# Attention stack of four layers on one core: four-head row tiles for the scores, column tiles for the sums over keys, the reciprocal of the denominators through DRAM, and the layers interleaved

## The chip, the cores and the metric

The kernel runs on one core of one Trainium2 chip. The metric is the device time in microseconds of one execution of the whole program. The engines are called PE (TensorE, matrix products), ACT (ScalarE), DVE (VectorE), POOL (GpSimd) and SP (SyncE, which here issues DMA transfers); "PEld" is PE's weight load. A matrix product has a stationary operand, the weights, and a moving one that is streamed past it.

The kernel before was run in every batch of experiments as well and gave 2697.99 to 2701.73 us in all of them, so times of different batches are compared here, but not differences of some 10 us and less.

## The reference, cut to what matters

There are 2048 tokens of width 512 and 32 heads of 16. Four layers follow each other, A, B, A, B, each on a normalised input and with a residual. A works on four segments of 512 tokens, causally, and adds a memory term; B attends to all keys.

```python
def _A_ref(x, wq, wk, wv, wo, beta):           # 4 segments s of L = 512 tokens
    phi = lambda t: jnp.where(t > 0, t + 1.0, jnp.exp(t))
    g = _sigmoid(beta).reshape(1, H, 1, 1)
    ...
    for s in range(N):
        qs, ks, vs = (q[:, :, s].copy(), k[:, :, s].copy(), v[:, :, s].copy())
        logits = jnp.einsum('bhqd,bhkd->bhqk', qs, ks) * scale + mask   # causal
        p = _softmax(logits, axis=-1)
        a_dot = jnp.einsum('bhqk,bhkd->bhqd', p, vs)
        pq = phi(qs)
        num = jnp.einsum('bhld,bhde->bhle', pq, M)
        den = jnp.einsum('bhld,bhd->bhl', pq, z)[..., None] + 1e-06
        o = g * (num / den) + (1.0 - g) * a_dot
        outs.append(o)
        pk = phi(ks)
        M = M + jnp.einsum('bhld,bhle->bhde', pk, vs)
        z = z + jnp.einsum('bhld->bhd', pk)
    ...
def _B_ref(x, wqkv, wo):
    ...
    scores = jnp.einsum('bhqd,bhkd->bhqk', q, k) * Dh ** (-0.5)
    p = _softmax(scores, axis=-1)
    o = jnp.einsum('bhqk,bhkd->bhqd', p, v)
...
x = x + _A_ref(_layernorm(x), ...); x = x + _B_ref(_layernorm(x), ...)   # twice
```

Softmax is taken without a maximum in both kernels: the exponential of all scores, the sum of exponentials times values, and a division by the sum of exponentials, which comes as a 17th column of the values, set to one.

## The kernel before: the parts that the change touches

Each layer is finished before the next begins. A head has only 16 of the 128 rows of a block of q, so the kernel masks q to one head and multiplies full 128-row blocks. The scores come out with keys on partitions and 512 queries on the free axis.

```python
    def qm_chunk(self, pair_idx, h, col0):           # q with all heads but h set to 0
        ...
        sc.add("dve", lambda e: e.tensor_scalar(dst, src, mcol, None, op0=ALU.mult), ...)

    KT_GROUPS = [[0, 1, 2], [3, 4, 5], [6, 7, 8], [9, 10, 11], [12, 13], [14, 15]]

    def b_unit(self, p, h, qc, g, slot_qm, c, uctr):
        ...
        for i, kt in enumerate(kts):                 # 3 or 2 blocks of 128 keys
            lhsT = self.kT[:, c, kt * 128:(kt + 1) * 128]
            out_ap = self.ps[:, bank.col0:bank.col0 + 512]
            sc.add("pe", ... e.matmul(out_ap, lhsT, qmap, start=True, stop=True) ...)
        ...
        sc.add("act", lambda e: e.activation(dst, src, ACT.Exp, scale=float(SCALE)), ...)
```

For the values, the exponentials are the weights: 128 keys by 128 queries are loaded, and only 17 columns are streamed. Queries then lie on partitions, so the reciprocal is of a small tile, 128x4.

```python
    def b_pv_part(self, p, h, qc, qt, state):
        ...
        for kt in range(16):
            lhsT = self.pT[:, col + qt * 128: col + (qt + 1) * 128]
            rhs = self.v_aug[:, kt, h * 17:(h + 1) * 17]
            out_ap = self.ps[:, col0 + qt * 17: col0 + (qt + 1) * 17]
            sc.add("pe", ... e.matmul(out_ap, lhsT, rhs, start=(kt == 0), stop=(kt == 15)) ...)

    def b_norm(self, p, h, qc, state):
        ...
        sc.add("dve", lambda e: e.reciprocal(sm[:, 0:4], den), ...)
        sc.add("dve", lambda e: e.tensor_tensor(dst, acc3[:, :, 0:16], rb, ALU.mult), ...)
```

The layers are built one after the other; the normalisation, the projections and, in A, the whole memory state come before the layer's first exponential.

```python
    def layer_A(self, li):
        self.ln_all(evac_eng=self.ln_evac_eng)
        for n in range(4):
            for g in self.proj_groups_A(n, nb_all):
                g()
        self.a_mem_init()
        ...                                          # a_nd_tile, a_deltaM: memory of all segments
        for s in range(NSEG):
            for h in range(H):
                info = self.a_pair(pair, s, h)       # scores, mask by a matmul, exponential
                if prev is not None:
                    self.a_pv_norm(prev)
                ...
```

## Time and profile before

| | before |
|---|---|
| time, median of 2 runs | 2701.17 us (2700.76 to 2701.58) |
| span of the profiled run | 2698.6 us |
| ACT busy | 2346.2 us (87%) |
| PE busy, instructions | 2085.3 us (77%), 26524 matmuls |
| mean granted PE clock | 0.965 |

The page gives the busy time of each engine with its share of the span and its number of instructions, then the span in 40 slices: each digit is the busy share of a slice in tenths, and for PEclk the granted clock in tenths of full speed. The page of the kernel before:

```profile
...
PE 2085.3 (77%) x26524; PEld 1242.5 (46%) x26976; DVE 777.9 (29%) x2571; ACT 2346.2 (87%) x2098; POOL 13.5 (1%) x19
...
PE   6788688777777777777786886887777777777777
...
ACT  6488658999999999999873886689999999999997
...
PEclk9799899999999999999977997999999999999998
...
```

ACT is at 9 tenths through both B layers and falls at the start of every layer. The groups by shape of the kernel before (line, engine, operation, output from input, shapes, count, then busy us, mean ns of one, and the idle time before them with what ended it):

```profile
...
L794 ACT ACTIVATE pT<-ps 128x1536 bf16<-128x1536 f32 x1024 | 1403.5, 1458 | 111.2 <-PE ps L786 89.4
...
L813 PEld LDWEIGHTS ps<-v_aug,pT 128*128 128x128 bf16 x16384 | 558.6, 96 | 244.5 <-ACT pT L794 1.7
L794 ACT ACTIVATE pT<-ps 128x1024 bf16<-128x1024 f32 x512 | 512.1, 1043 | 0.1
L729 ACT ACTIVATE pT<-ps 128x1280 bf16<-128x1280 f32 x256 | 308.3, 1237 | 123.2 <-PE ps L720 119.2
...
```

The exponentials take 1403.5 + 512.1 + 308.3 = 2224 us: that is the floor of this design on ACT. The 16384 value products each load 128 columns of weights to stream 17. Where ACT has no exponential is read from its timeline, in which each line has its start, its length and in brackets the idle time before it and what ended that (`x6` joins six in a row):

```profile
...
126.35 1.24 ACT L729 ACTIVATE pT<-ps 128x1280 bf16<-128x1280 f32 x1 [34.80 <-PE ps L720]
...
361.41 7.57 ACT L794 ACTIVATE pT<-ps 128x1536 bf16<-128x1536 f32 x6 [20.06 <-PE ps L786]
...
1468.35 1.24 ACT L729 ACTIVATE pT<-ps 128x1280 bf16<-128x1280 f32 x1 [37.02 <-PE ps L720]
...
```

The first exponential starts at 126.35 us. B's first one, at 361.41 us, comes 55 us after the last of A, which ended near 306 us, and A's second layer begins after 131 us without exponentials. Together with the same places in the second half and the end these are about 389 us. The table of stretches (start:end, length, then the busy time of PE, PEld, DVE, ACT and POOL in this order, each with its count, the granted clock, the DMA share and GB/s) says the same of whole stages, the first A layer and the middle of B:

```profile
...
0.00:337.00 337.00, 254.31 (x2867) 158.24 (x2916) 244.16 (x817) 230.46 (x276) 13.53 (x19) 0.92 0.06 20
540.00:1000.00 460.00, 354.14 (x4887) 211.00 (x4966) 54.63 (x202) 450.40 (x370) 0.00 (x0) 1.00 0.01 2
...
```

B is bound by ACT, 450.40 of 460 us. The A layer is not: 230.46 of 337 us.

### The profile page before, as it was taken

The page shows a single profiled execution, that of the slowest core. Times are in us where ns is not written, and L with a number is a line of the kernel's source. Part 1 is how long each engine was busy: PE and PEld are TensorE (multiplying, and loading weights), DVE is VectorE, ACT ScalarE, POOL GpSimd, SP SyncE. Part 2 cuts the span into 40 slices and gives each one's busy share as a digit, 9 for nine tenths or more (in the row PEclk, how much of TensorE's full clock was granted, in tenths as well). Part 3 has the DMA queues.
Part 4 walks back from the last instruction along what each step waited for, and adds up shares of the span by engine and source line. Part 5 has one row for each costly group of instructions (what it writes and reads, how often), then busy time and mean ns, then how long its engine had stood idle before and what let it go on. Part 6 is the DMA issues. An engine that isn't in the chain of part 4 may idle for free.

```text
span 2698.6 us, 62409 instructions
## 1 busy us (share of the span) xinstructions
PE 2085.3 (77%) x26524; PEld 1242.5 (46%) x26976; DVE 777.9 (29%) x2571; ACT 2346.2 (87%) x2098; POOL 13.5 (1%) x19
## 2 busy tenths in 40 slices
PE   6788688777777777777786886887777777777777
PEld 2465444444444444444434654444444444444444
DVE  6777732111111111111177776321111111111111
ACT  6488658999999999999873886689999999999997
POOL 1000000000000000000000000000000000000000
PEclk9799899999999999999977997999999999999998
DMA  2000000000000000000000000000000000000000
GB/s 71 24 2 2 1 1 1 25 1 2 1 2 2 1 2 2 2 2 2 1 1 24 2 2 1 1 1 2 2 1 9 2 2 9 2 1 2 9 2 9
DMA packets 9919, 15.56 MB, mean 6 GB/s; under 512 B 432, under 2 KB 8624, under 8 KB 9648
## 3 DMA queue, kind: packets, MB, share of 16 engines
q1 hardware_dynamic: 9648, 11.54, 1.3%
q8 instruction: 219, 3.59, 0.5%
q14 instruction: 52, 0.43, 0.0%
HBM read 9.45 MB, written 2.10 MB: 4 GB/s over the span
## 4 chain that ended last, share of the span: by engine, by line
ACT 51%; PE 29%; issue 14%; DVE 5%; DMA 0%; ACTq 0%; SPq 0%
ACT pT L794 44%; PE ps L786 11%; ACT pT L729 5%; PE ps L495 4%; PE ps L715 3%; PE ps L864 3%; PE ps L510 2%; PE ps L749 2%; PE ps L720 2%; PE ps L813 1%; PE ps L465 1%; DVE xn_ring L458 1%; DVE amem L664 1%; DVE lnst L444 1%; PE ps L843 1%
## 5 line engine op out<-in xcount | busy, mean ns | idle before, releaser
L794 ACT ACTIVATE pT<-ps 128x1536 bf16<-128x1536 f32 (+1 forms) x1536 | 1879.1, 1320 | 111.3 <-PE ps L786 89.4
L786 PE MATMUL ps<-qm,kT 128*128 128x512 bf16 x3750 | 1049.0, 377 | 443.5 <-ACT pT L794 359.5
L813 PEld LDWEIGHTS ps<-v_aug,pT 128*128 128x128 bf16 x16384 | 558.6, 96 | 244.5 <-ACT pT L794 1.7
L786 PEld LDWEIGHTS ps<-qm,kT 128*128 128x128 bf16 x4096 | 301.8, 96 | 771.1 <-PE ps L813 344.3
L813 PE MATMUL ps<-v_aug,pT 128*128 128x17 bf16 x16384 | 562.9, 171 | 1.5 <-ACT pT L794 1.5
L827 DVE RECIPROCAL small<-ps 128x4 f32<-128x4 f32 x256 | 46.9, 183 | 1500.6 <-PE ps L813 1500.6
L729 ACT ACTIVATE pT<-ps 128x1280 bf16<-128x1280 f32 x256 | 308.3, 1237 | 123.2 <-PE ps L720 119.2
L715 PE MATMUL ps<-qm,kT 128*128 128x384 bf16 (+3 forms) x948 | 204.2, 294 | 0.6 <-DVE small L757 0.6
L686 DVE TENSOR_SCALAR qm<-qT,blockmask_f 128x512 bf16<-128x512 bf16 x512 | 177.9, 350 | 88.6 <-PE ps L786 88.6
L720 PE MATMUL ps<-negmask,ident 128*128 128x128 bf16 x1024 | 184.1, 220 | 10.6 <-DVE qm L686 5.6
L749 PE MATMUL ps<-v_aug,pT 128*128 128x17 bf16 x2560 | 104.7, 172 | 38.9 <-ACT pT L729 37.4
L715 PEld LDWEIGHTS ps<-qm,kT 128*128 128x128 bf16 x1024 | 99.9, 98 | 57.5 <-DVE qm L686 5.4
L495 PE MATMUL ps<-xT,wproj 128*128 128x512 bf16 x502 | 122.6, 397 | 1.4 <-PE ps L465 0.9
L749 PEld LDWEIGHTS ps<-v_aug,pT 128*128 128x128 bf16 x2560 | 82.1, 96 | 84.4 <-ACT pT L729 83.9
L720 PEld LDWEIGHTS ps<-negmask,ident 128*128 128x128 bf16 x1024 | 100.2, 98 | 2.8
L465 PE MATMUL ps<-ident,xn_ring 128*128 128x128 bf16 x256 | 38.2, 308 | 64.0 <-DVE xn_ring L458 64.0
L510 PE MATMUL ps<-wproj,xT 128*128 128x512 bf16 x376 | 84.3, 379 | 0.6 <-DVE phqT L543 0.2
L495 PEld LDWEIGHTS ps<-xT,wproj 128*128 128x128 bf16 x512 | 52.3, 103 | 65.9 <-issue 11.1
L768 DVE SCALAR_TENSOR_TENSOR tok<-tmpo,gcol,amem 128x64 bf16<-128x64 f32 x256 | 73.0, 285 | 9.1
L757 DVE RECIPROCAL small<-ps 128x4 f32<-128x4 f32 x256 | 46.8, 183 | 81.7 <-PE ps L749 71.7
L472 ACT ACTIVATE xT<-ps 128x512 bf16<-128x512 bf16 x64 | 37.7, 598 | 31.5 <-PE ps L465 31.5
L868 DVE TENSOR_TENSOR x_tok<-x_tok,ps 128x512 bf16<-128x512 bf16 x64 | 43.9, 686 | 66.3 <-PE ps L864 66.3
(60 smaller groups left out, 845.7 us busy)
## 6 DMA issues: line engine op xcount, KB each, us to landing
wproj<-in_B_wqkv_dram SPq DMA_DIRECT2D x2, 1536.0 KB, 6.7
x_tok<-in_A_x_dram SPq DMA_DIRECT2D x4, 512.0 KB, 5.6
out_dram<-x_tok SPq DMA_DIRECT2D x4, 512.0 KB, 2.9
wproj<-in_A_wq_dram SPq DMA_DIRECT2D x2, 512.0 KB, 6.0
wproj<-in_A_wk_dram SPq DMA_DIRECT2D x2, 512.0 KB, 7.0
wproj<-in_A_wv_dram SPq DMA_DIRECT2D x2, 512.0 KB, 7.6
woA<-in_A_wo_dram SPq DMA_DIRECT2D x1, 512.0 KB, 8.9
woB<-in_B_wo_dram SPq DMA_DIRECT2D x1, 512.0 KB, 8.9
```

Source lines behind the costliest of these rows:

```text
L495: sc.add("pe", (lambda lhsT, rhs, cin: lambda e: e.matmul(self.ps[:, bank.col0:bank.col0 + 512], lhsT, rhs, start=(cin == 0), stop=(cin == ...
L510: sc.add("pe", (lambda lhsT, rhs, cin: lambda e: e.matmul(self.ps[:, bank.col0:bank.col0 + 512], lhsT, rhs, start=(cin == 0), stop=(cin == ...
L686: sc.add("dve", lambda e: e.tensor_scalar(dst, src, mcol, None, op0=ALU.mult), reads=[self.b_qT[c][n + i] for i in range(4)] + [self.b_blo ...
L715: sc.add("pe", (lambda out_ap, lhsT, rhs: lambda e: e.matmul(out_ap, lhsT, rhs, start=True, stop=False))(out_ap, lhsT, rhs), reads=[kreads ...
L720: sc.add("pe", (lambda mask_out: lambda e: e.matmul(mask_out, self.ident[:], self.negmask[:], start=False, stop=True))(mask_out), reads=[s ...
L729: sc.add("act", lambda e: e.activation(dst, src, ACT.Exp, scale=float(SCALE)), writes=gr, bank_ops=[(B0, "r", alloc), (B1, "r", alloc), (B ...
L749: sc.add("pe", (lambda out_ap, lhsT, rhs, kb, qb: lambda e: e.matmul(out_ap, lhsT, rhs, start=(kb == 0), stop=(kb == qb)))(out_ap, lhsT, r ...
L768: sc.add("dve", lambda e: e.scalar_tensor_tensor(dst, tmpo, omg, am, op0=ALU.mult, op1=ALU.add), reads=[b_tmpo, self.b_gcol] + [self.b_ame ...
L786: sc.add("pe", (lambda out_ap, lhsT: lambda e: e.matmul(out_ap, lhsT, qmap, start=True, stop=True))(out_ap, lhsT), reads=[self.b_kT[c][kt] ...
L794: sc.add("act", lambda e: e.activation(dst, src, ACT.Exp, scale=float(SCALE)), writes=gr, bank_ops=[(banks[i], "r", alloc) for i in range( ...
L813: sc.add("pe", (lambda out_ap, lhsT, rhs, kt: lambda e: e.matmul(out_ap, lhsT, rhs, start=(kt == 0), stop=(kt == 15)))(out_ap, lhsT, rhs, kt),
L864: sc.add("pe", (lambda lhsT, rhs, c: lambda e: e.matmul(self.ps[:, bank2.col0:bank2.col0 + 512], lhsT, rhs, start=(c == 0), stop=(c == NCH ...
```

## The change

The intent is to fill those 389 us. The scores and the value products are rearranged so that PE needs fewer and better filled instructions, and then everything that is not an exponential, for this block or the next layer, is cut into small tasks ("fills") that are put between the exponentials.

Scores: four heads occupy four groups of 32 rows, and four products run side by side in row tiles. Since a head has 16 rows, q is kept twice, once with the even and once with the odd heads set to zero. Values: the weights are now the 17 columns of v, the exponentials are streamed 512 wide, and four heads lie in four column tiles. Queries are on the free axis, so a denominator is one row of 512; it is sent to DRAM, brought back as 128x32 for the reciprocal, sent out again and brought back repeated over 16 partitions. The causal mask is no longer a matmul but a select on POOL after the exponential.

The diff replaces nearly the whole file; this is its core.

```diff
-            lhsT = self.kT[:, c, kt * 128:(kt + 1) * 128]
-            sc.add("pe", ... e.matmul(out_ap, lhsT, qmap, start=True, stop=True) ...)
+            lhsT = self.kB[32 * g:32 * g + 32, c, kt * 128:(kt + 1) * 128]
+            rhs = self.q[32 * g:32 * g + 32, slot, G.e, c, :]
+            sc.add("pe", lambda e: e.matmul(self.ps[:, b0:b0 + 512], lhsT, rhs, start=True, stop=True, tile_position=(32 * g, 0)), ...)
...
-            lhsT = self.pT[:, col + qt * 128: col + (qt + 1) * 128]
-            rhs = self.v_aug[:, kt, h * 17:(h + 1) * 17]
+        o = self.ps[32 * g:32 * g + DH + 1, G.acc * 512 + q0:G.acc * 512 + 512]
+        self.sc.add("pe", lambda e: e.matmul(o, lhsT, rhs, start=first, stop=last, tile_position=(0, 32 * g), skip_group_check=True), ...)
...
-        sc.add("dve", lambda e: e.reciprocal(sm[:, 0:4], den), ...)
+        self.at(1, d1)               # num -> DRAM, denominator rows only
+        self.at(1 + gap, d2)         # DRAM -> rc, 128x32
+        self.at(1 + 2 * gap, rec)    # reciprocal of 128x32 on DVE
+        self.at(2 + 2 * gap, d3)     # rc -> DRAM
+        self.at(2 + 3 * gap, d4)     # DRAM -> rb, each row to 16 partitions
+        self.at(2 + 5 * gap, mul)    # oT = num * rb; after 8 of them the block is done
...
+    def phi(self, o, bk, dst, bdst, name):
+        sc.add("act", lambda e: e.activation(t, o, ACT.Exp), ...)
+        sc.add("pool", lambda e: e.tensor_scalar(t, t, 1.0, None, op0=ALU.min), ...)
+        sc.add("dve", lambda e: e.scalar_tensor_tensor(dst, o, 0.0, t, op0=ALU.max, op1=ALU.add), ...)
...
+                def den(c=c):        # memory denominator, for 4 blocks c of each segment
+                    sc.add("pe", lambda e: e.matmul(o, self.Zb[:, c, :], self.phq[:, c, :], start=True, stop=False), ...)
+                    ...
+                    i = self.rot("r_rm", 1)                       # one buffer rm
+                    sc.add("dve", lambda e: e.reciprocal(self.rm[:, i, :], o), ...)
+                    sc.add("pool", lambda e: e.tensor_tensor(self.phq[:, c, :], self.phq[:, c, :], self.rm[:, i, :], ALU.mult), ...)
+                def mem(c=c):
+                    sc.add("pe", lambda e: e.matmul(o, self.Mb[:, c, :], self.phq[:, c, :], start=True, stop=True), ...)
...
+    def run_units(self, kind, tiles, est):
+            for tile, bi in zip(unit, banks):                     # 2 tiles in A, 3 in B
+                self.scores(tile, bi)
+            sc.add("act", ... e.activation(dst, src, ACT.Exp, scale=float(SCALE)) ...)
+            if unit[0][0] != "B":
+                self.causal(unit, s0)                             # select on POOL
+            self.drain_pv(self.LAG)                               # value products of earlier units
+            ...
+            budget = max(est, left / n_left if self.spread else est)
+            while self.fills and budget > 0:
+                t = self.fills.pop(0)
+                budget -= t.cost + 0.25
+                t.run()
...
+                    if qc == 0:
+                        self.fills += [t for c in range(1, NCH) for t in self.tB[layer]["k"][c]]
```

## The prediction

> **What bounds the kernel now.** ScalarE's exponentials. The page: ACT busy 2346 of 2699 us (87%); costliest groups the B exponentials (1403.5 us for 1024 of 128x1536, 512.1 us for 512 of 128x1024) and A's (308.3 us for 256 of 128x1280). In the stretch table ACT is busy 450 of 460 us in mid-B, but about 230 of 337 us in each A layer; six B exponentials (8192 columns) take 7.43 us in the timeline. The ScalarE timeline shows where no exponential runs: 0-126, about 306-361, 1337-1468, 1648-1706 and 2680-2699 us: about 389 us of normalisation, projections and memory state, on the chain of waits through PE and DVE. That can be won; the exponentials (2224 us) stay.
>
> **What the change does.**
> 1. B exponentials become 683 per layer of 128x1536. At an estimated 1.38 us start to start (from the 7.43) that is 942 us per layer against 951. A: 160 of 128x1024 per layer, about 0.95 us, 152 us against 154. Together 2190 us of exponentials. The Trainium skill ("ScalarE: Activation LUTs", What ACT_TABLE_LOAD costs) gives one element per cycle at 1.2 GHz and a 93 ns overlap; the trace agrees.
> 2. Other ACT work (masked q, phi, memory, sums, layer-norm copies): about 110 per A layer of 0.59 us: 65 us, 130 us in all.
> 3. PE: before, 16384 B value matmuls each needed a 128-column weight load (96 ns). After, scores are 32-row tiles and values 17-column tiles, 2048+2048 per B layer, each streaming 512 columns. The skill ("TensorE: Matmul & The Clock Gate", Part 3) gives 3.07x for four row tiles, 2.38x for three column tiles; no trace here shows it yet. A 512-column matmul lasts 377 ns here, so I estimate 0.4-0.5 us for a unit's three scores and the same for its values: about 0.9 us, below 1.38. So B stays ACT-bound, with stalls where projections (4 matmuls, about 1 us) are put in.
> 4. A segments: PE about 40 units x 0.8 + 35-40 us of filling work = 65-72 us, ACT 55 us, DVE about 46 us (four 128x512 reciprocals, 3-4 us each by the trace's 183 ns for 4 and 353 ns for 32 elements), GpSimd 35-40 us. So A is PE-bound: about 265 us per layer.
> 5. The 1/denominator bounce is about 16 chains per layer, off the critical path except at A-to-B changes, where the last block's chain, output projection, normalisation and keys stay exposed (about 16 us each), and at the end.
>
> **Sum (estimate).** Exponentials 2190 + other ACT 130 + start 36 + two changes 32 + tail 25 + A's PE excess over ACT 95 + B stalls 25 = about 2530 us. About 300 of the 389 us are hidden; part comes back as ACT and PE work inside A.
>
> **Predicted: 2530 us, 8 in 10 between 2420 and 2650.** Faster by over 2%: 0.84; within 2%: 0.11; slower by over 2%: 0.05.
>
> **What would show it.** Exponentials about 2190 us busy. B layers: ACT 96% or more busy, about 955 us each; its idle in 1 us pieces around projections. A layers: ACT about 80%, released by PE scores. Score matmuls of one unit start within some ns of each other. No exponential-free stretch over 30 us except at start and end. PE clock near 1.
>
> **What would make it wrong.** Row or column tiles that do not overlap, or drains at each change of tiling: PE then needs more than 1.38 us per unit and B becomes PE-bound (2700 and more). A lower granted clock with partly filled arrays. GpSimd masking or DVE reciprocals holding A. DMA chains longer than their steps.

## The result, and the profile after

| | before | after |
|---|---|---|
| time, median of 2 runs | 2701.17 us | 2848.40 us (2847.5 to 2849.3) |
| span of the profiled run | 2698.6 us | 2845.8 us |
| ACT busy | 2346.2 us | 2281.1 us |
| PE busy, matmuls | 2085.3 us, 26524 | 2288.1 us, 12232 |
| POOL busy | 13.5 us | 375.5 us |
| mean granted PE clock | 0.965 | 0.624 |

A ratio is computed as the mean time of one kernel's runs over that of the other's of the same rounds, so it is not quite the ratio of the medians quoted. Here it is 1.0549, 95% interval 1.0518 to 1.058: the change made the kernel slower by 5.5%. The prediction, 2530 us, was wrong in its direction.

The page after:

```profile
...
PE 2288.1 (80%) x12232; PEld 518.4 (18%) x12232; DVE 572.0 (20%) x870; ACT 2281.1 (80%) x1910; POOL 375.5 (13%) x690
...
PE   5667786888888888878868668678888888888886
...
ACT  3546464999999899879956447479989998999995
...
PEclk8667788555655655665568777885555556555555
...
```

ACT is no longer bare at the layer boundaries, but in the A layers (slices 1 to 6 and 21 to 26) it stands at 3 to 7 tenths. The granted clock is 5 or 6 tenths in the B layers.

The groups by shape after:

```profile
...
L832 ACT ACTIVATE pT<-ps 128x1536 bf16<-128x1536 f32 x1356 | 1832.8, 1791 | 95.0 <-PE ps L628 95.0
L628 PE MATMUL ps<-q,kB 32*128 32x512 bf16 x4096 | 807.3, 582 | 254.7 <-ACT pT L832 250.3 <-DVE kB L399 0.5
...
L832 ACT ACTIVATE pT<-ps 128x1024 bf16<-128x1024 f32 x334 | 341.3, 1042 | 219.0 <-PE ps L639 211.0 <-PE ps L628 5.4
...
L509 DVE RECIPROCAL rm<-ps 128x512 f32<-128x512 f32 x24 | 80.6, 3358 | 29.0 <-PE ps L639 22.1 <-POOL phq L510 6.9
...
L456 POOL TENSOR_SCALAR tph<-tph 128x512 bf16<-128x512 bf16 x48 | 71.5, 1490 | 319.6 <-ACT tph L455 319.4
...
```

B's exponentials wait 95.0 us in all, A's 219.0 us, of which 211.0 us ended with a score product of A (L639). The rest of A's lost time is between exponentials, in other ACT work that waits too. The reciprocals of the memory denominators (L509) last 3358 ns, the minimum of `phi` on POOL (L456) 1490 ns.

The table of stretches, for the first A layer, 70 us of steady B, and the second A layer:

```profile
...
48.00:420.00 372.00, 283.30 (x1620) 83.79 (x1616) 164.08 (x237) 213.70 (x262) 169.96 (x316) 0.74 0.07 23
550.00:620.00 70.00, 60.09 (x315) 10.72 (x315) 3.81 (x6) 70.00 (x53) 0.00 (x0) 0.50 0.03 9
1441.00:1819.00 378.00, 283.65 (x1622) 84.51 (x1620) 162.45 (x224) 207.86 (x252) 164.01 (x300) 0.77 0.08 24
...
```

In the steady stretch of B, ACT is busy 70.00 of 70 us, although the granted clock is 0.50. In the A layers no engine is full: PE 283.30 of 372 us, ACT 213.70, DVE 164.08, POOL 169.96. That looks like a stage bound by waits in order; the experiments test it.

Taking the layers from the first to the last exponential after, and to the last residual before, the difference of spans falls like this:

| | before | after | difference |
|---|---|---|---|
| start and first A | 0 to 317.5 | 0 to 421.3 (first exponential at 48.1) | +104 |
| first B | 317.5 to 1352.0 | 421.3 to 1440.2 | -16 |
| second A | 1352.0 to 1662.2 | 1440.2 to 1819.4 | +69 |
| second B and end | 1662.2 to 2698.6 | 1819.4 to 2845.8 (last exponential to 2816.5) | -10 |
| all | 2698.6 | 2845.8 | +147 |

Eight lines of the timeline after show what an A segment does while its memory term is built (PE, ACT and DVE lines chosen):

```profile
...
94.18 3.36 DVE L509 RECIPROCAL rm<-ps 128x512 f32<-128x512 f32 x1 [1.23 <-PE ps L639]
...
98.14 0.61 PE L639 MATMUL ps<-q,kA 32*128 32x256 bf16 x4
...
98.86 1.02 ACT L832 ACTIVATE pT<-ps 128x1024 bf16<-128x1024 f32 x1 [1.57 <-PE ps L639]
98.91 3.36 DVE L509 RECIPROCAL rm<-ps 128x512 f32<-128x512 f32 x1 [1.37 <-PE ps L639]
...
102.41 0.58 PE L518 MATMUL ps<-phq,Mb 128*128 128x512 bf16 x1 [3.13 <-DVE rm L509]
...
102.93 0.61 PE L639 MATMUL ps<-q,kA 32*128 32x512 bf16 x2
...
103.60 1.02 ACT L832 ACTIVATE pT<-ps 128x1024 bf16<-128x1024 f32 x1
103.64 3.36 DVE L509 RECIPROCAL rm<-ps 128x512 f32<-128x512 f32 x1 [1.37 <-PE ps L639]
```

The exponential at 98.86 us has its scores from 98.14. The next exponential starts at 103.60, because its scores start at 102.93, because PE had the memory product L518 in front of them, and that waited 3.13 us for the reciprocal that began at 98.91. By the code, that reciprocal was still reading the one of two spare PSUM banks that L518 was to fill. PE's later products did not go around the one that waited. The reciprocals follow each other in 4.73 us: 3.36 for itself, 1.16 for POOL's product that frees the single buffer `rm`, and the semaphores. The exponential of such a unit lasts 1.02 us.

The change from the first A to the first B layer:

```profile
...
420.48 4.06 SPq L699 DMA_DIRECT2D dscr<-num  x2
...
421.26 1.45 ACT L832 ACTIVATE pT<-ps 128x1536 bf16<-128x1536 f32 x1 [0.43 <-PE ps L628]
...
425.73 0.32 SPq L704 DMA_DIRECT2D rc<-dscr  x1
...
427.81 2.31 SPq L713 DMA_DIRECT2D dscrb<-rc  x2
...
435.84 0.61 PE L764 MATMUL ps<-woA,oT 128*128 128x512 bf16 x1 [10.83 <-DVE oT L732]
...
457.45 1.42 PE L424 MATMUL ps<-xT,wB 128*128 128x512 bf16 x4 [0.69 <-ACT xT L397]
...
459.50 1.45 ACT L832 ACTIVATE pT<-ps 128x1536 bf16<-128x1536 f32 x1 [2.11 <-PE ps L628]
...
```

After one exponential of B at 421.26 us there is none until 459.50. The last chunk of A goes to DRAM at 420.48, its product reaches PE at 435.84 (about 15 us for the four transfer steps and the reciprocal), and then come output projections, normalisation, transposes and a key projection in one chain of more than 20 us. The second A-to-B change costs 40 us in the same way.

Two more bare stretches lie inside the second A layer, of 25.3 us and, from 1688.7 us on, of 28.7 us. The ACT lines of the first:

```profile
...
1578.48 1.02 ACT L832 ACTIVATE pT<-ps 128x1024 bf16<-128x1024 f32 x1 [1.56 <-PE ps L639]
1598.15 0.60 ACT L397 ACTIVATE xT<-ps 128x512 bf16<-128x512 bf16 x1 [18.64 <-PE ps L386]
...
1604.80 1.03 ACT L832 ACTIVATE pT<-ps 128x1024 bf16<-128x1024 f32 x1
...
```

In each of them the trace shows the last steps of the memory chain and then the output projection and the whole normalisation of a finished block, without an exponential in between. By the code, the memory products of the third and fourth segment ask for that block at once. At the same places of the first A layer about 10 us are bare. No run here changed this order.

Lastly, one place in B where a fill was put in:

```profile
...
721.67 3.13 PE L764 MATMUL ps<-woB,oT 128*128 128x512 bf16 x8
...
724.74 0.39 PE L628 MATMUL ps<-q,kB 32*128 32x512 bf16 x3
...
725.23 1.45 ACT L832 ACTIVATE pT<-ps 128x1536 bf16<-128x1536 f32 x1 [2.00 <-PE ps L628]
...
```

The fill, an output projection of eight products, lasts 3.13 us at the clock of that moment; the scores come after it, and ACT waits 2.00 us.

### The profile page after: what moved, and what is told of

The parts are those of the page before. It is cut to its first block, busy times and chain, and to the rows that moved or that the text cites. A ratio compares the mean times of both kernels' runs of the same rounds, so it can differ in the third digit from the quotient of the medians.

```text
span 2845.8 us, 30885 instructions
## 1 busy us (share of the span) xinstructions
PE 2288.1 (80%) x12232; PEld 518.4 (18%) x12232; DVE 572.0 (20%) x870; ACT 2281.1 (80%) x1910; POOL 375.5 (13%) x690
## 4 chain that ended last, share of the span: by engine, by line
ACT 44%; PE 24%; issue 18%; DVE 7%; POOL 5%; DMA 2%; ACTq 0%; SPq 0%; DVEq 0%; POOLq 0%
ACT pT L832 41%; PE ps L424 6%; PE ps L764 6%; PE ps L673 4%; PE ps L628 3%; PE ps L639 3%; POOL tph L456 2%; DVE rm L509 2%; PE ps L435 2%; DVE q L447 2%; POOL pT L873 1%; POOL phq L510 1%; ACT tph L455 1%; ACT q L444 1%; DVE x L766 1%
## 5 line engine op out<-in xcount | busy, mean ns | idle before, releaser
L832 ACT ACTIVATE pT<-ps 128x1536 bf16<-128x1536 f32 (+1 forms) x1690 | 2168.6, 1643 | 314.0 <-PE ps L639 211.0
L628 PE MATMUL ps<-q,kB 32*128 32x512 bf16 x4096 | 807.3, 582 | 254.7 <-ACT pT L832 250.3
L673 PE MATMUL ps<-pT,vB 128*17 128x512 bf16 x4096 | 805.3, 576 | 3.5 <-ACT pT L832 2.8
L628 PEld LDWEIGHTS ps<-q,kB 32*128 32x128 bf16 x4096 | 143.9, 98 | 936.7 <-ACT pT L832 884.7
L873 POOL TENSOR_SCALAR_AFFINE_SELECT pT<-pT 128x256 bf16<-128x256 bf16 (+1 forms) x448 | 206.2, 464 | 425.7 <-ACT pT L832 415.4
L673 PEld LDWEIGHTS ps<-pT,vB 128*17 128x17 bf16 x4096 | 133.9, 91 | 576.4 <-issue 543.5
L673 PE MATMUL ps<-pT,vA 128*17 128x384 bf16 (+3 forms) x1024 | 156.9, 371 | 38.3 <-ACT num L397 19.5
L639 PE MATMUL ps<-q,kA 32*128 32x128 bf16 (+3 forms) x1024 | 160.2, 370 | 4.4 <-ACT pT L832 4.4
L424 PE MATMUL ps<-xT,wA 128*128 128x512 bf16 x256 | 85.4, 471 | 35.6 <-DVE phq L457 32.3
L456 POOL TENSOR_SCALAR tph<-tph 128x512 bf16<-128x512 bf16 x48 | 71.5, 1490 | 319.6 <-ACT tph L455 319.4
L424 PE MATMUL ps<-xT,wB 128*128 128x512 bf16 x256 | 86.1, 471 | 20.9 <-DVE q L447 14.1
L509 DVE RECIPROCAL rm<-ps 128x512 f32<-128x512 f32 x24 | 80.6, 3358 | 29.0 <-PE ps L639 22.1
```

What stands on the lines that cost most here:

```text
L424: self.sc.add("pe", (lambda lhsT, rhs, k: lambda e: e.matmul(o, lhsT, rhs, start=(k == 0), stop=(k == NCH - 1)))(lhsT, rhs, k), reads=[bw[ ...
L456: sc.add("pool", lambda e: e.tensor_scalar(t, t, 1.0, None, op0=ALU.min), reads=[bt], writes=[bt], name=f"phm{name}")
L509: sc.add("dve", lambda e: e.reciprocal(self.rm[:, i, :], o), reads=[bk], writes=[self.b_rm[i]], name=f"mrec{s}_{c}")
L628: sc.add("pe", lambda e: e.matmul(self.ps[:, b0:b0 + 512], lhsT, rhs, start=True, stop=True, tile_position=(32 * g, 0)), reads=[self.b_kB[ ...
L639: sc.add("pe", (lambda lhsT, rhs, g, n, col: lambda e: e.matmul(self.ps[:, b0 + col:b0 + col + n], lhsT, rhs, start=True, stop=True, tile_ ...
L673: self.sc.add("pe", lambda e: e.matmul(o, lhsT, rhs, start=first, stop=last, tile_position=(0, 32 * g), skip_group_check=True), reads=read ...
```

## The experiments

The theory: the A layers cost too much because the memory chain goes PE, ACT, POOL, DVE, PE, DVE, POOL, PE in order, with long steps and single buffers, and every step of it stands in PE's queue in front of the scores. In B, the cost is the fills and the changes of layer. The rivals: (R1) the halved clock makes PE the bound; (R2) row and column tiles do not overlap, or changing between them is dear; (R3) the bounce through DRAM delays everything that needs it.

The runs came in three batches of four, in the order 1 to 4, 5 to 8 and 9 to 12; the kernel before took 2701.73, 2699.97 and 2699.22 us in them. All but the last kernel were run once (state unknown), so differences of some 10 us and less are not leant on.

### 1. The matmuls alone, and what halves the clock

This kernel keeps the shapes and drops the rest (its result is wrong): full products, four row tiles, four column tiles and alternating groups of three, each in a steady stream; then score and value products paced by exponentials of 128x1536 as in B, with variations.

```diff
+        self.s1_full(); self.warm()                    # 180 products 128x128 by 512
+        self.s2_row(); self.warm()                     # 640 in four row tiles
+        self.s3_col(); self.warm()                     # 640 in four column tiles of 17
+        self.s4_alt(); self.warm()                     # 100 times 3 row, 3 column
+        self.paced(60, "row", "col", 0); self.warm()   # as in B
+        self.paced(60, "row", "col", 1); self.warm()   # and one full product per unit more
+        self.paced(60, "row", "col", 2); self.warm()
+        self.paced(60, "full", "col", 0); self.warm()
+        self.paced(60, "row", "full", 0); self.warm()
+        self.paced(60, "full", "full", 0); self.warm()
```

> A kernel with a wrong output on purpose: stretches of matmuls of one kind, each stretch begun with the array warm (60 full 128x128 matmuls of 512 columns between stretches). Theory CLOCK (the new shapes, at the duty they have here, let the granted TensorE clock fall to half): the full stretch keeps 1.0; the stretch paced by exponentials (3 scores of 32 rows, 3 sums of 17 columns per 1.35 us) falls to about 0.5 as in the B layers of the changed kernel (0.50 to 0.57 there). If it is the tile shape as such, the unpaced row-tile and column-tile stretches fall too; if it is the duty, they stay near 1.0, and one or two extra full matmuls a unit raise the paced one to 1.0. Theory DRAIN (each change of tiling empties the array): the unpaced alternation takes clearly more than 0.25 us + 0.25 us per group of 3 + 3, about 0.65 us, at the full clock. Rival to CLOCK: the paced stretch keeps 1.0 and the clock of the changed kernel falls for another reason.

Measured: the kernel took 819.2 us. Its table of stretches, with the same columns but no DVE, for the full products, the row tiles, the alternation, the pace of B, and the pace of B with two full products more:

```profile
...
25.00:64.00 39.00, 38.79 (x178) 17.68 (x181) 0.00 (x0) 0.00 (x0) 1.00 0.00 0
77.00:111.00 34.00, 34.00 (x632) 16.06 (x636) 0.00 (x0) 0.00 (x0) 1.00 0.01 2
...
172.00:237.00 65.00, 65.00 (x602) 19.34 (x602) 0.00 (x0) 0.00 (x0) 1.00 0.01 1
262.00:331.00 69.00, 58.44 (x308) 10.66 (x306) 69.00 (x52) 0.00 (x0) 0.50 0.00 1
...
454.00:523.00 69.00, 62.77 (x400) 15.68 (x405) 69.00 (x52) 0.00 (x0) 1.00 0.00 1
...
```

Whole groups give 180 full products in 39 us, 0.216 us each, and 640 row tiles in 34.71 us, 0.054 each: four run in the time of one. The column tiles gave the same 34.71 us. In the alternation a group of three, which would take 0.216 us if nothing were lost, takes 0.324 us. The 0.11 us more are put down to the change of tiling; groups of three without a change were not run. So R2 falls: PE's work for a unit of B is about 0.65 us at full clock, under the 1.345 us of an exponential.

At the pace of B the clock falls to 0.50, and the 60 exponentials still follow each other every 1.34 us. With two full products more per unit, or with full score or value products, the clock stays at 1.00; with one more it was 0.5 for 20 us and then 1.0. Tiles alone, in a steady stream, kept 1.00. So it is not the shape of the tiles as such but how much work PE gets: 0.65 of 1.345 us, about 48% counted at full clock, was too little, and 0.97 of 1.345 us, about 72%, was held in the end (0.65 and, as an estimate, 0.216 for the extra product and 0.11 for one more change of tiling). Where between these the limit lies was not measured, nor tiles alone at a share between 48% and 100%. At the halved clock PE is busy for 58.44 of 69 us, and the clock still does not come back, so a busy share that is read after the fall does not show the lack. Gaps in PE's work were at most 0.63 us, apart from one at the start of each of these stretches (0.9 to 1.4 us), which those that kept 1.00 had too; so it was no long pause either.

### 2. Without the reciprocals of the memory term

The four reciprocals of 128x512 per segment become copies. Its output is wrong, which doesn't matter for the time.

```diff
-  e.reciprocal(self.rm[:, i, :], o)
+  e.tensor_copy(self.rm[:, i, :], o)
```

> Wrong result on purpose: the 24 reciprocals of 128x512 on VectorE (3.36 us each) become copies (about 0.69 us). Theory WAITS (the A layers are long because PE waits in order behind VectorE and GpSimd): the A layers lose most of 24 x 2.67 = 64 us, so about 2785 us. Theory CLOCK (A is PE work at a clock of 0.74): only the part that lies on the chain of waits goes (6% of 400 us per layer, about 20 us each at most), so 2810 to 2845 us, unless the shorter waits also raise the clock.

Measured: 2794.69 us, 54 less than after. The A layers went from 372 and 378 us to 348 and 351; the B layers stayed (1017 and 997). The reciprocals are 80.6 us busy in all, and a copy of such a tile takes about 0.69 us, so some 64 us of DVE time were taken away, and 51 of them were won in A. These reciprocals were on the critical path most of the time.

### 3. The minimum of phi on DVE

```diff
-        sc.add("pool", lambda e: e.tensor_scalar(t, t, 1.0, None, op0=ALU.min), ...)
+        sc.add("dve", lambda e: e.tensor_scalar(t, t, 1.0, None, op0=ALU.min), ...)
```

> Right result: the 48 minima of phi (1.49 us each on GpSimd) move to VectorE. Theory WAITS: GpSimd's minimum is 6.7% of the chain of waits in the first A layer, so about 25 us per A layer goes, 2800 us. Theory CLOCK: 10 to 30 us at most, 2820 to 2840 us.

Measured: 2793.88 us, 55 less than after, and correct; the A layers 352 and 357 us. The group by shape of this kernel:

```profile
...
L456 DVE TENSOR_SCALAR tph<-tph 128x512 bf16<-128x512 bf16 x48 | 14.2, 296 | 50.5 <-ACT tph L455 50.5
...
```

The same minimum takes 296 ns on DVE, 1490 on POOL. That is 1.19 us less for each of 48, 57 us in all, and 42 us of it show in A. So this operation on POOL took five times its length on DVE (spans on POOL are rough in the profile, but the 55 us of the run agree with it), and its place in the chain made it count.

### 4. Full clock in all layers

One full product, with an unused result, ahead of the scores of every unit that follows one without a fill.

```diff
+            if not self.filled:
+                for bi in banks[:NDUM]:
+                    self.dummy(bi)
```

> Right result: one extra full-array matmul of 512 columns ahead of a unit's scores, in units that follow one without filling work (its result is overwritten). Theory CLOCK: the granted clock rises well above 0.62, stalls around projections in B shrink, A gets shorter; 2650 to 2800 us. If one is not enough to hold the clock it only costs PE time at half clock, where B has 0.13 us of slack a unit: B becomes PE-bound at about 1.9 us a unit, and the time goes above 3200 us. Theory WAITS: no gain.

Measured: 2848.93 us, nothing won, with a mean clock of 0.920. In the B layers the clock was 0.97 and 0.99, and they took 1016 and 989 us (1019 and 997 after). In the A layers it changed little, 0.74 and 0.81, with 386 and 378 us. So the low clock of B by itself cost some 11 us; R1 falls for B as it stands, and is untested for A by this run.

### 5. A without its waits

Reciprocals as copies, and the minimum, POOL's product and the causal select left out; in A the output does not wait for the bounced reciprocal. Its output is wrong, which doesn't matter for the time.

```diff
-        sc.add("pool", lambda e: e.tensor_scalar(t, t, 1.0, None, op0=ALU.min), ...)
-        sc.add("dve", lambda e: e.reciprocal(self.rm[:, i, :], o), ...)
-        sc.add("pool", lambda e: e.tensor_tensor(self.phq[:, c, :], ..., self.rm[:, i, :], ALU.mult), ...)
+        sc.add("dve", lambda e: e.tensor_copy(self.rm[:, i, :], o), ...)
-                self.causal(unit, s0)
+                    rb = self.onesb[:, :]
```

> Wrong result on purpose: in the A layers all work of VectorE and GpSimd that PE was seen to wait for is made short or left out (the 128x512 reciprocals become copies, no minimum in phi, no product with the reciprocal on GpSimd, no causal mask, the product with 1/denominator does not wait for its DMA). PE's and ScalarE's work stays as it is. Theory WAITS (PE's waits in order, which also let the clock fall): each A layer falls from 372 and 378 us to about 265 to 290 us with a granted clock above 0.9 in it; in all about 2650 us. Theory CLOCK (the clock falls in A because units of tiled matmuls alone do not keep it, whatever the waits): the A layers keep a clock below 0.8 and stay above 320 us each; in all above 2730 us.

Measured: 2678.13 us, and the A layers about 305 and 311 us, between the expectations: 67 us per A layer less than after, but not the predicted 265. The clock in A was 0.84 and 0.82, against 0.74 and 0.77 after, so part of the 67 us probably came through the clock: PE's busy time fell by about 30 and 20 us, its idle time by the rest. The bare stretches at the A-to-B changes were still 30.1 and 29.4 us (36.8 and 39.1 after), although A's output no longer waited for the bounce: the transfers are the smaller part of them. The table of stretches of this kernel, inside the first A layer:

```profile
...
45.00:335.00 290.00, 240.42 (x1517) 77.58 (x1540) 124.37 (x232) 198.54 (x248) 25.18 (x60) 0.84 0.08 27
...
```

PE is busy 240.42 of 290 us, ACT 198.54. PE is the busiest, as predicted, but it is still idle for about a sixth of the time.

### 6. Both parts of A mended, correctly

The minimum on DVE. The denominators of a segment's 32 heads are collected in 32 rows by four accumulating products, so that one reciprocal of 32x512 does for four of 128x512; a product with a matrix of zeros and ones spreads it over the 128 rows, and the multiplication moves from POOL to DVE. Its tasks are put behind the next keys' projections.

```diff
+                for c in range(NCH):
+                    sc.add("pe", ... e.matmul(o, self.Zb[:, c, :], self.phq[:, c, :], start=(c == 0), stop=False) ...)
+                ...
+                        return e.reciprocal(self.rmb[:, :], o[0:32, :])
+                ...
+                    sc.add("pe", lambda e: e.matmul(o, self.sel[:, c * 128:(c + 1) * 128], self.rmb[:, :], start=True, stop=True), ...)
+                    sc.add("dve", lambda e: e.tensor_tensor(self.phq[:, c, :], self.phq[:, c, :], o, ALU.mult), ...)
-                    sc.add("dve", lambda e: e.reciprocal(self.rm[:, i, :], o), ...)
-                    sc.add("pool", lambda e: e.tensor_tensor(self.phq[:, c, :], ..., self.rm[:, i, :], ALU.mult), ...)
```

> Right result: the minimum of phi on VectorE; one reciprocal of 32x512 per segment instead of four of 128x512, spread to the 128 rows by a matmul with a 0/1 matrix, and the product on VectorE from PSUM. The two single changes took 54 and 55 us off; WAITS: together about 90 to 110 us, so 2740 to 2760 us, A layers about 325 us each. If both had shortened the same wait, only 55 to 65 us: 2785 us.

Measured: 2726.17 us, 122 less than after; the A layers 324 and 320 us, the B layers as they were (1008 and 997). Of its groups by shape, the reciprocals:

```profile
...
L518 DVE RECIPROCAL rmb<-ps 32x512 bf16<-32x512 f32 x6 | 20.1, 3346 | 15.1 <-PE ps L663 15.1
...
```

One reciprocal of 32x512 takes as long as one of 128x512 (3346 and 3358 ns), so the time goes by the elements along the free axis, and packing heads into rows saves three of four. This kernel has both exact fixes and wins 48 and 59 us in the A layers, of the 67 that leaving everything out had won. In the second A layer about half of the 59 us comes from the two bare stretches shown above, 54 us together: over 12 us only one is left, of 20.6 us. What the new order of tasks did beside the shorter steps was not run apart.

### 7. A quicker bounce at the end of A

The last pair of A sends its steps without a pause between them (one unit apart in place of three).

```diff
-        gap = self.gap
+        gap = 1 if (G.kind == "A" and G.blk == 3 and G.c == NCH - 1) else self.gap
```

> Right result: as combo, and for the last pair of heads of an A layer the steps between the DMAs of the 1/denominator bounce are 1 unit instead of 3. The exponential-free stretch at each A-to-B change was 38 and 40 us; if the step delays make it, each falls to 15 to 25 us, in all 30 to 50 us less than combo. If the bounce itself or the output projection and normalisation behind it make it, less than 10 us in all.

Measured: 2730.17 us, 4 more than combo. The miss is informative: the pauses do not set the change from A to B. What stands in the way is then the order of what comes after the bounce, which experiment 9 tests.

### 8. Both remedies for B

On combo_quick: the extra product in B, and a credit that spreads the fills, so that a fill that overdraws the budget is paid for by later units without one.

```diff
+            if self.mode == "B" and not self.filled:
+                for bi in banks[:NDUM]:
+                    self.dummy(bi)
...
+            if self.mode == "B":
+                self.credit = min(self.credit, 0.0) + 2.0 * left / n_left if self.credit < 0 else 2.0 * left / n_left
+                budget = self.credit
...
+            if self.mode == "B":
+                self.credit = budget
```

> Right result: as combo_quick, and in B one extra full matmul per unit without filling work, to hold the clock, and the filling work spread over the layer instead of one piece in each unit until it is gone. The B layers took 1019 and 997 us, of which 683 x 1.345 = 919 is exponentials and 38 to 40 the change; the rest, 62 and 38 us, are stalls around filling work. If those come from filling work at half clock and in a row, most of it goes: 60 to 90 us less than combo_quick, about 2640 us. If the clock in B does not matter and spreading only moves the stalls, less than 20 us.

Measured: 2659.16 us, 71 less than combo_quick; the B layers 973 and 963 us in place of 1006 and 1000. Its exponentials of B, from the groups by shape:

```profile
...
L860 ACT ACTIVATE pT<-ps 128x1536 bf16<-128x1536 f32 x1356 | 1829.4, 1611 | 33.3 <-PE ps L653 33.1
...
```

The waits before these exponentials fell from 86.6 us (combo_quick; 95.0 after) to 33.3.

### 9. The order of the key projections

On combo_quick: B's remaining keys by token block and not by column block.

```diff
-  self.fills += [t for c in range(1, NCH) for t in self.tB[layer]["k"][c]]
+  self.fills += [self.tB[layer]["k"][c][n] for n in range(4) for c in range(1, NCH)]
```

> Right result: combo_quick, with only the order of B's filling key projections changed: by token block, so that those of the last block come last. In combo_quick the exponential-free stretch at an A-to-B change is 38 us, as before the step delays were cut, because the fourth piece of filling work asks for the keys of the last token block and forces the whole chain of the last A block to be waited for in place. If that is the cause, 16 units can run in the meantime: each stretch falls from 38 to under 20 us, in all 35 to 60 us less than combo_quick's 2730. If the bounce is simply exposed, no change.

Measured: 2693.77 us, 36 less than combo_quick; the B layers 989 and 982 us, 17 and 18 less each. The old order asked for the fourth token block of the second column block as its fourth fill; that block is A's last one, so the request forced the whole rest of A's chain into the queues at once, with nothing to do beside it. In the new order the first nine fills need only tokens that are done.

### 10. Spreading alone

On combo_quick: the credit of experiment 8 without the extra product.

> Right result: combo_quick with the filling work of B spread over the layer, without the extra matmuls, so at half clock. combo_all (both) took 71 us off; the extra matmuls alone, on the changed kernel, took 3 and 8 us off its two B layers and 0 in all. If spreading alone does it: about 2665 to 2680. If it takes both (at half clock a piece of filling work overruns its unit however it is spread): 2700 to 2720.

Measured: 2739.59 us, 9 more than combo_quick and above both expectations. Its exponentials of B:

```profile
...
L856 ACT ACTIVATE pT<-ps 128x1536 bf16<-128x1536 f32 x1356 | 1832.6, 1555 | 105.3 <-PE ps L652 105.2
...
```

So spreading alone wins nothing (105.3 us of waits), the clock alone won 3 and 8 us in the B layers (experiment 4, on the kernel after; its B exponentials waited 79.4 us), and both together won 71 us. These waits leave out the idle time before ACT's other work: in the faster kernel of experiment 9 they were 116.7 us. The times of the layers decide. At half clock a fill such as the 3.13 us one does not fit into a unit that has 1.345 us, of which the tiles take 1.2 (three scores 0.61 and three value products 0.60 in the timeline of steady B), however it is spread; at full clock, fills in a row add up. That sentence is the reading of the traces, not a run by itself.

### 11. A without its waits, at a higher clock

Experiment 5 with the extra product in A. Its output is wrong, which doesn't matter for the time.

```diff
+            if self.mode == "A" and not self.filled:
+                for bi in banks[:NDUM]:
+                    self.dummy(bi)
```

> Wrong result on purpose: nowait, with one extra full matmul ahead of the scores of those A units that follow one without filling work. In nowait the A layers took 304 and 311 us at a granted clock of about 0.85, PE busy 83%. If the clock is what keeps them above the 265 predicted: the clock goes above 0.93 and the layers to 275 to 290 us. If PE's work and the hand-overs between PE and ScalarE are, the extra matmuls only add work: 305 to 330 us.

Measured: 2660.65 us; the A layers 299 and 303 us, between the expectations, with the clock at 0.90 and 0.91. So this much more clock, with the extra products' own time in it, was worth some 6 and 8 us of an A layer, no more than single runs can tell apart. About 35 us per layer over the predicted 265 remain. The stretch inside the first A layer:

```profile
...
45.00:335.00 290.00, 243.36 (x1581) 81.03 (x1609) 125.22 (x232) 202.47 (x255) 25.18 (x60) 0.90 0.09 29
...
```

PE is still idle for about a sixth of the time. In the first A layer its longest waits in sum are for the masked memory sums that DVE prepares (Zb, 11.6 us), for the normalised input from DVE (8.4), for ACT's copies of the value sums (7.9) and for DVE's step of phi (6.3). In the second, two bare stretches like those shown above, of 15.1 and 18.4 us, are left and make up most of the remaining 35 us. None of these was changed by a run: they stay open.

### 12. The version that the experiments point to

combo_quick with the key order, the credit, and the extra product except around fills.

```diff
...
+            will = any(not t.done for t in self.fills) and self.credit > 0
+            if self.mode == "B" and not self.filled and not will:
+                for bi in banks[:NDUM]:
+                    self.dummy(bi)
...
+  self.fills += [self.tB[layer]["k"][c][n] for n in range(4) for c in range(1, NCH)]
```

> Right result: combo_quick with the key order of korder, filling work spread, and the extra matmul only in units that neither have nor follow filling work. Sum: combo_all's 2659 less 35 to 60 us for the two changes and about 15 us of the stalls of 0.66 us that a unit with both an extra matmul and filling work had: about 2600 us, ratio to before 0.96 to 0.97.

Measured: 2652.59 us, median of 4 runs (2649.91 to 2659.95), against 2699.22 us of the kernel before in the same rounds (7 runs); ratio 0.9836, interval 0.9819 to 0.9852. It is correct and 1.6% below the kernel before; and the expected gain over combo_all did not come: its single run of 2659.16 us lies within the four. The traces show why. Add up, over B, by how much the starts of neighbouring exponentials lie more than 1.345 us apart. In the first 100 us of the two B layers this is 98 us in combo_quick, 82 in combo_all, 67 in korder and 66 in best: the key order and the two remedies shorten the same stretch, and their gains were added up as if they did not. After the first 100 us it is 90 us in combo_quick, 43 in combo_all and 49 in best. Leaving out the extra product around fills did not help there: in the first B layer the clock was 0.95 in place of 1.00 and about 9 us came back, in the second it held and 4 us were won.

## Why the prediction was right or wrong

The sum can be set against the layers of the trace, term by term. B's exponentials were predicted as 2 times 942 us; A's part is 304 of exponentials, 130 of other ACT work and 95 of PE excess.

| term | predicted | measured | difference |
|---|---|---|---|
| A layers, 304 + 130 + 95 | 529 | 372 + 378 = 750 | +221 |
| B exponentials, start to start | 1884 | 1847 | -37 |
| B stalls | 25 | 91 | +66 |
| two A-to-B changes | 32 | 38 + 40 = 78 | +46 |
| start and end | 61 | 48 + 29 = 77 | +16 |
| sum | 2531 | 2843 | +312 |

B's 1847 us is the busy time of the 1356 full exponentials, 1832.8 us, and of 14 smaller ones; its stalls are the remainder of the two B layers, 1019 + 997 - 1847 - 78 us.

**The step that failed is step 4, "So A is PE-bound: about 265 us per layer".** Each engine's work in an A segment had been costed by itself (65 to 72 us of PE, 46 of DVE, 35 to 40 of POOL), and the largest was taken for the time of the segment. The sizes were not far off: PE was busy for 283 us per layer, 71 per segment (at a clock of 0.74 to 0.77 and not near 1, so that the agreement is partly luck), DVE for 164, 41 per segment, POOL for 170, 42 per segment, and the reciprocals were 3.36 us as estimated. What failed is the maximum: the engines do not work side by side there. The memory chain runs from one engine to the next, has single buffers, and its PE steps stand in order ahead of the scores. Experiment 5 took the waits away and won 67 us per layer; experiments 2 and 3 each won 20 to 27 us of it by one step of the chain, and experiment 6 won 48 and 59 with a correct kernel. Of the excess of 107 and 113 us per layer, 67 went with the waits, the rise of the clock that came with it included; more clock on top gave some 6 and 8 us (experiment 11), and about 35 us stay open. The prediction named "GpSimd masking or DVE reciprocals holding A" among what would make it wrong, but did not price a chain, nor the 1.49 us of a minimum on POOL.

**"B stalls 25" was mis-sized**: 91 us. It took both the full clock and the spreading of fills to win most of them back (experiments 4, 8, 10): the first alone won 3 and 8 us, the second alone nothing, both 71.

**"Two A-to-B changes 32" was mis-sized**: 78 us. The prediction gave about 16 us to each change for everything: the bounce, the projection, the normalisation and the keys. The bounce alone took about 15 us, and the rest came after it in one chain of more than 20 us, called in early by the order of the key projections. Experiment 9 won 17 and 18 us by that order, and experiment 7 nothing by a quicker bounce. Without any wait for the bounce in A the bare stretches were still 30.1 and 29.4 us (experiment 5). R3 falls as the main cause: the transfers are a part of the change, but not the larger one.

**"PE clock near 1" was wrong**: 0.56 to 0.58 in B and 0.74 to 0.77 in A. In steady B this was harmless, since the tiles need about 1.2 us of 1.345 even at half clock. It did take away the room for fills.

**Right** were the exponentials (2168.6 us busy against 2190, a little less because one unit takes 1.345 us and not 1.38; the Trainium skill's one element per cycle at 1.2 GHz, in "ScalarE: Activation LUTs", What ACT_TABLE_LOAD costs, gives an estimate of 1.28 us for 1536 elements, and the trace agrees within 5%); that ACT is full in steady B (174.46 of 180 us from 2120 to 2300); that four row tiles overlap, 4.0 times in a steady stream (experiment 1) against the 3.07 times of "TensorE: Matmul & The Clock Gate", Part 3; and that the start would shrink (126 to 48 us; the end grew from 18 to 29 us). The 7.43 us of the prediction for six exponentials are 7.34 us in the trace from the first start to the last end, and 7.45 us from group to group; nothing hangs on this.

Where did the expected gain of 170 us go? The bare stretches were filled: of 389 us, 155 are left (48 + 78 + 29). But the A layers took 221 us more than predicted, mostly as new waits in order, 54 us of it in the two bare stretches of the second A layer, and B stalled for 66 us more than predicted.

## What to carry to other kernels

When work is interleaved into a stage, cost the stage as a chain, in the order in which each engine's queue is issued, and not as the largest of the engines' sums: a long step on a side engine (a 3.36 us reciprocal, a 1.49 us minimum) held everything that the matrix engine had queued behind its consumer, and a cheaper engine or a shorter step was worth about three quarters of the time that it saved (51 of 64 us and 42 of 57 show in the A layers). A second buffer was not tried. Before trusting a plan that leaves the matrix engine half idle, check the granted clock: fills sized at full clock may not fit at half of it. When two remedies each win next to nothing, try them together before both are dropped; and when two remedies each win something, see whether they shorten the same stretch before adding up their gains.

## What the Trainium skill lacked or had wrong

- "TensorE: Matmul & The Clock Gate", Why this matters for your kernels: it asks for no idle gaps over about 3 us. Here the clock stayed at 0.50 with gaps of at most 0.63 us, and of 1.4 us once at the start, with work for about 48% of the time at full clock; it held 1.00 with two full products more per 1.345 us. The page says elsewhere that the clock follows how busy PE has been, and that short pauses between groups can lower it, but gives no share of time at which it does.
- The same page, Part 3, Measured speedup vs the span model: it gives 3.07 times for four row tiles and 2.38 for three column tiles of 512. In a steady stream four row tiles and four column tiles of 17 both gave 0.054 us each against 0.216, that is 4.0 times.
- "TensorEngine Tiling (Array Packing)", Key Properties: it says that a change of tiling mode drains the engine, without a figure. Here groups of three in turn took 0.324 us against 0.216, which makes about 0.11 us per change at full clock, if all of it is the change.
- "GPSIMD Engine Reference", 4.1 Engine selection: one-input elementwise work is called roughly line-rate. A minimum with a constant on 128x512 bf16 took 1490 ns on GpSimd and 296 ns on VectorE. The two-input product was nearer to what the page says (about 2 times): 1242 ns against 683 with one operand in PSUM.
- "VectorE: DVE Perf Modes", First, the fixed hardware budget: it says that the reciprocal is an iterative division with a repeat count of 8, without a time. Here 512 elements per partition took 3358 ns on 128 partitions and 3346 on 32, about 6.5 ns per element along the free axis.
